# Attention and two gated layers on one core: folded weights of batches 4 to 7 made per head through DRAM, the attention pool split in two, Silu written with Tanh

## The chip, the cores and the metric

The kernel runs on 1 core of one Trainium2 chip. The metric is device time in microseconds (us), the median of several runs; the profile is one execution of the same program with its own time.

## The reference, cut to what matters

```
a    = softmax over the sequence of phi            # 8 batches, 8 heads, 576 positions, 32 memories
k_m, v_m = a^T k, a^T v                            # per head 32 x 64
attn = softmax(q k_m^T / 8) ; x = attn v_m         # per head 576 x 64
x = (silu(x @ w_gate) * (x @ w_val)) @ w_out       # 4608 x 512, 512 x 1536, 1536 x 512
h = x @ w_in ; g = where(h > 0, h, exp(min(h,0)) - 1)
out = g @ w_out2                                   # 512 x 2048, 2048 x 512
```

All is float32; weights arrive as float64.

## The kernel before, in words

**Precision.** Each matrix is split in a high and a low part (`fp32r`), and each product is three matmuls: high by high, high by low, low by high.

**Folding.** The kernel never forms x. For each batch and each pair of 128-column units p (0 to 5) of the first layer, `vw` (L112) multiplies the batch's `v_m` (block-diagonal, transposed: `vt`) by the gate and value columns `WG[p]`. That takes two groups g of six matmuls with 512 columns, one PSUM tile each, then a copy (L124) and a difference (L125) into `VW[b, p]`. `gate1` and `val1` (L148, L155) multiply `VW` by the attention matrix `at`, 288 positions at a time: six matmuls of 288 columns each.

**Loop 1** (L406) goes over the 8 batches with units u = 0 to 3 (p = 0, 1) and writes the partial result `p1` of the down product to DRAM. Between its matmuls `tick` gives out tasks of a list: the front of the attention of batch b+2 (k_m and v_m), the back of batch b+1 (scores, softmax, transposes), and `vw` of batch b+1. Everything of the attention lies in one pool, `at_p`, which is closed after iteration 6, when the pools `wb` and the PSUM of loop 2 are opened and the weights of p = 2 to 5 and of u = 4 to 11 are asked for (L440 to L457).

**Loop 2** (L512) goes over the 8 batches and two halves with units u = 4 to 11: `gate1`, `val1`, the down product of the unit two before (`down2`), and one piece of `vw` of the next batch from `vwq`. Each half ends with an addition to `p1` and a store to DRAM. Late in loop 2 the weights of the third part are asked for (L527, L534, L540 to L543).

**Part 3** (L594) is the last layer: 9 tiles of 512 tokens by 16 units, each 24 matmuls of 512 columns, with Exp and Tanh on ScalarE (L568, L569).

**A weight load** (`load_w`, L92) is a DMA of 512 KB and the splitting of float64 in two float32 parts (`split_w`, L71): two ScalarE copies (L77, L83), four VectorE operations (L78, L79, L81, L82) and two GpSimd operations (L84, L85). The raw tile `wr` and the value `v` have two buffers, the integer tile `c` has one:

```
v = wt_p.tile([128, 512], F32, tag="wv", name="wv", bufs=2)
c = wt_p.tile([128, 512], I32, tag="wc", name="wc")
```

**Order.** The order of the text is a priority: a scheduler with a timeline of its own places each instruction when its inputs and its buffer are there, so work can run ahead of its place in the text. All DMAs are issued from the one queue of SP, in order. A buffer in a pool is given out in turn, and the next tile in it waits for the readers of the last one.

Of the kernel before, what the change touches and what calls it, by code (L numbers as in the profile page):

```python
# [26 lines left out]
UA = 4  # L27
NCH = 5
NWA = 24
NWB = 32  # L30
NWC = 8
# [3 lines left out]
def attention_moe_moe(ctx: ExitStack, tc: tile.TileContext, qT, phiT, kv, w1g, w1o, w2, out):  # L35
# [10 lines left out]
    wt_p = ctx.enter_context(tc.tile_pool(name="wt", bufs=1))  # L46
# [14 lines left out]
    ps_at = st_ps.enter_context(tc.tile_pool(name="ps_at", bufs=2, space=PSUM))  # L61
    st_at = ExitStack()
    at_p = st_at.enter_context(tc.tile_pool(name="at", bufs=1))
# [3 lines left out]
    p1_d = [dram.tile([128, KD, S], F32, name=f"p1d{b}") for b in range(B)]  # L67
    x1_d = [dram.tile([128, KD, S], F32, name=f"x1d{b}") for b in range(B)]


    def split_w(raw, hi, lo):  # L71
        lo32, hi32 = raw[:, :, 0], raw[:, :, 1]
        v = wt_p.tile([128, 512], F32, tag="wv", name="wv", bufs=2)
# [74 lines left out]
    def gate1(b, u, at, s0):  # L148
        pg = ps_gv.tile([128, HS], F32, tag="g", name="pg")
        up1(pg, VW[b, u // 2], 256 * (u % 2), at, s0)  # L150
        s = t_p.tile([128, HS], F32, tag="s", name="s")
        act(out=s, in_=pg, func=AF.Silu)  # L152
        return s

    def val1(b, u, at, s0, s):  # L155
# [3 lines left out]
        tt(out=h, in0=s, in1=pv, op=ALU.mult)  # L159
# [3 lines left out]
    ident = at_p.tile([128, 128], F32, tag="ident", name="ident")  # L163
    make_identity(nc, ident)
    mask = at_p.tile([128, 4, 64], F32, tag="mask", name="mask")
# [14 lines left out]
    class Batch:  # L180
# [21 lines left out]
        def phi(self):  # L202
            ph = self.ph
            nmx = at_p.tile([128, 2], F32, tag="nmx", name="nmx")
            nc.vector.tensor_reduce(out=nmx, in_=ph, op=ALU.max, axis=AX.X, negate=True)
            sm = at_p.tile([128, 2], F32, tag="sm", name="sm")
# [3 lines left out]
            self.rs = at_p.tile([128, 2], F32, tag="rs", name="rs", bufs=2)  # L210
# [41 lines left out]
        def kv_out(self):  # L252
            self.kvm = at_p.tile([128, 2, 2, 256], F32, tag="kvm", name="kvm")
# [5 lines left out]
        def k_T(self):  # L259
# [4 lines left out]
            self.kT = at_p.tile([128, 2, 2, 128], F32R, tag="kT", name="kT")  # L264
# [26 lines left out]
        def score(self, c):  # L291
            n = chunk(c)
            if c == 0:
                self.sc = at_p.tile([128, NCH, 256], F32, tag="sc", name="sc")
# [6 lines left out]
            t = at_p.tile([128, 4, 64], F32, tag="sct", name="sct", bufs=2)  # L301
# [103 lines left out]
    wl = []  # L405
# [231 lines left out]
```

## Time and profile before

| | |
|---|---|
| time, median of 3 runs | 1793.68 us (1787.94 to 1795.11) |
| the profiled execution | 1791.92 us |
| its span, first to last instruction | 1790.1 us |
| TensorE matmul busy | 95% of the span |
| VectorE, ScalarE, GpSimd busy | 59%, 43%, 16% |
| mean granted clock of TensorE | 0.971 |

Busy time of TensorE is a sum over matmuls that overlap in the pipeline, so a matmul's own duration is longer than the time until the next one starts. Where an engine runs without a gap, the number of matmuls in a stretch says more than its busy share.

### The profile page before, as it was taken

To read this page: it belongs to the slowest core of one execution; us is meant where nothing else is said; L and a number is where in the kernel's file an instruction comes from. 1 tells how busy PE (TensorE), PEld (TensorE's weight loads), DVE (VectorE), ACT (ScalarE), POOL (GpSimd) and SP (SyncE) were. 2 spreads that over 40 slices of the span, in tenths; PEclk is the share of its full clock that TensorE was granted. 3 is DMA by queue.
4 is the path that set the end of the run, shared out by engine and by line. 5 is a ranking of instruction groups with operands and counts; after the bars stand their busy time and mean duration, and the time that the engine had idled before them with its cause. 6 is when DMAs were issued, how large, how long until landed. Compare 5 with 4: busy or idle time off the path is not lost.

```text
span 1790.1 us, 24102 instructions
## 1 busy us (share of the span) xinstructions
PE 1708.9 (95%) x9424; PEld 1496.5 (84%) x9424; DVE 1047.8 (59%) x1781; ACT 770.8 (43%) x1447; POOL 277.6 (16%) x197
## 2 busy tenths in 40 slices
PE   6689999999869999999999999999999999999998
PEld 4478998898759999999999878888888888888887
DVE  6887677657665333333368887455545555555554
ACT  5567666654433222322345444343434343434332
POOL 3552222114442000000034441000000000000000
PEclk8779999999969999999999999999999999999999
DMA  6555444234434121112225221010101010101000
GB/s 217 181 183 192 155 158 155 65 116 148 139 104 166 54 66 66 67 52 79 67 75 169 92 83 48 1 48 0 48 1 48 1 48 1 47 1 47 1 24 24
DMA packets 68209, 144.68 MB, mean 81 GB/s; under 512 B 7168, under 2 KB 38912, under 8 KB 66048
## 3 DMA queue, kind: packets, MB, share of 16 engines
q1 hardware_dynamic: 68096, 143.16, 24.1%
q8 instruction: 73, 1.20, 0.3%
q14 instruction: 40, 0.33, 0.1%
HBM read 101.19 MB, written 41.94 MB: 80 GB/s over the span
## 4 chain that ended last, share of the span: by engine, by line
PE 78%; DVE 9%; DMA 4%; ACT 3%; issue 2%; POOL 2%; SPq 0%; ACTq 0%; POOLq 0%; DVEq 0%
PE acc L581 7%; PE acc L582 7%; PE acc L583 7%; PE pu L557 7%; PE pu L555 6%; PE pu L556 6%; PE acc L139 3%; PE acc L138 3%; PE acc L137 3%; PE pg L132 2%; PE pv L132 2%; PE pg L133 2%; PE pg L134 2%; PE pv L134 2%; PE pv L133 2%
## 5 line engine op out<-in xcount | busy, mean ns | idle before, releaser
L581 PE MATMUL acc<-whi,hh 128*128 128x512 f32 x576 | 224.8, 390 | 3.3 <-ACT hh L143 3.3
L555 PE MATMUL pu<-x1s,whi 128*128 128x512 f32 x576 | 224.2, 389 | 1.6 <-DVE g L571 1.6
L582 PE MATMUL acc<-wlo,hh 128*128 128x512 f32 x576 | 224.2, 389 | 0.0
L557 PE MATMUL pu<-x1s,wlo 128*128 128x512 f32 x576 | 224.1, 389 | 0.0
L556 PE MATMUL pu<-x1s,whi 128*128 128x512 f32 x576 | 224.1, 389 | 0.0
L583 PE MATMUL acc<-whi,hl 128*128 128x512 f32 x576 | 223.0, 390 | 0.0
L570 DVE SCALAR_TENSOR_TENSOR g<-e,g 128x512 f32<-128x512 f32 x144 | 104.8, 727 | 157.1 <-ACT g L569 156.9
L84 POOL TENSOR_TENSOR wv<-wv,whi 128x512 f32<-128x512 f32 x68 | 102.1, 1501 | 587.3 <-ACT whi L83 469.6
L143 ACT ACTIVATE hh<-g 128x512 fp32r<-128x512 f32 x144 | 90.9, 632 | 217.0 <-DVE g L571 212.4
L159 DVE TENSOR_TENSOR h<-s,pv 128x288 f32<-128x288 f32 x192 | 86.5, 451 | 164.5 <-PE pv L134 135.3
L568 ACT ACTIVATE e<-g 128x512 f32<-128x512 f32 x144 | 90.8, 631 | 205.5 <-DVE g L567 205.2
L138 PE MATMUL acc<-hh,wlo 128*128 128x288 f32 x512 | 151.7, 298 | 2.7 <-POOL wlo L85 2.7
L145 DVE TENSOR_TENSOR hl<-g,hh 128x512 fp32r<-128x512 f32 x144 | 100.3, 697 | 87.0 <-ACT hh L143 87.0
L139 PE MATMUL acc<-hl,whi 128*128 128x288 f32 x512 | 149.7, 298 | 0.7 <-DVE hl L145 0.7
L137 PE MATMUL acc<-hh,whi 128*128 128x288 f32 x512 | 150.1, 296 | 0.3 <-ACT hh L143 0.3
L145 DVE TENSOR_TENSOR hl<-h,hh 128x288 fp32r<-128x288 f32 x192 | 108.4, 565 | 61.7 <-ACT hh L143 61.2
L143 ACT ACTIVATE hh<-h 128x288 fp32r<-128x288 f32 x192 | 85.0, 443 | 124.4 <-DVE h L159 123.9
L152 ACT ACTIVATE s<-pg 128x288 f32<-128x288 f32 x192 | 78.1, 408 | 123.6 <-PE pg L134 122.6
L581 PEld LDWEIGHTS acc<-whi,hh 128*128 128x128 f32 x576 | 108.1, 188 | 27.8 <-ACT hh L143 5.7
L567 DVE TENSOR_SCALAR g<-pu 128x512 f32<-128x512 f32 x144 | 99.3, 689 | 53.5 <-PE pu L557 53.3
L555 PEld LDWEIGHTS pu<-x1s,whi 128*128 128x128 f32 x576 | 108.1, 188 | 24.3 <-DVE g L571 2.0
L583 PEld LDWEIGHTS acc<-whi,hl 128*128 128x128 f32 x576 | 107.9, 187 | 24.5 <-DVE hl L145 2.2
(107 smaller groups left out, 4084.1 us busy)
## 6 DMA issues: line engine op xcount, KB each, us to landing
kvr<-kv SPq DMA_DIRECT2D x32, 512.0 KB, 3.9
wr<-w SPq DMA_DIRECT2D x32, 512.0 KB, 3.5
wr<-w1g SPq DMA_DIRECT2D x24, 512.0 KB, 3.6
atd<-at SPq DMA_DIRECT2D x8, 1152.0 KB, 4.9
p1d<-p SPq DMA_DIRECT2D x64, 144.0 KB, 2.0
p1l<-p1d SPq DMA_DIRECT2D x16, 576.0 KB, 4.1
at<-atd SPq DMA_DIRECT2D x8, 1152.0 KB, 5.2
x1d<-p1l SPq DMA_DIRECT2D x16, 576.0 KB, 3.3
```

Source lines behind the costliest of these rows:

```text
L137: mm(ps, lhsT=w[0][:, ms], rhs=hs[0], start=start, stop=False)
L138: mm(ps, lhsT=w[1][:, ms], rhs=hs[0], start=False, stop=False)
L139: mm(ps, lhsT=w[0][:, ms], rhs=hs[1], start=False, stop=stop)
L143: act(out=hh, in_=h, func=AF.Copy)
L145: tt(out=hl, in0=h, in1=hh.bitcast(F32), op=ALU.subtract)
L555: mm(ps, lhsT=wh[:, k, :], rhs=xh, start=k == 0, stop=False)
L556: mm(ps, lhsT=wh[:, k, :], rhs=xl, start=False, stop=False)
L557: mm(ps, lhsT=wl[:, k, :], rhs=xh, start=False, stop=k == KD - 1)
L570: stt(out=g, in0=e, scalar=1.0, in1=g, op0=ALU.add, op1=ALU.mult)
L581: mm(accs[c], lhsT=hs[0][:, cs], rhs=wh, start=u == 0, stop=False)
L582: mm(accs[c], lhsT=hs[0][:, cs], rhs=wl_, start=False, stop=False)
L583: mm(accs[c], lhsT=hs[1][:, cs], rhs=wh, start=False, stop=u == NU2 - 1)
```

## The change

Three things are done.

1. **Per-head folding for batches 4 to 7** (`NM` = 4). In loop 2 the folded weights of batches 0 to 3 are made as before. For batches 4 to 7, one matmul makes those of all four batches for one head (64 rows of the weights): the 128 columns of the stationary side are 4 batches by 32 memories, and the 128 rows are the head's 64 rows twice, once against the high and once against the low part of the weights. A second matmul adds the low part of `v_m` by the high part of the weights. `load_vq` gathers `v_m` from DRAM in 48 DMAs with runs of 128 bytes, `load_wf` builds the stacked weights with four DMAs from SBUF to SBUF, `fold` makes the two matmuls, a copy and a store to DRAM, and `load_vw` reads the folded weights back, one DMA for each batch and p, and splits them.
2. **Pools.** The attention pool becomes `fr_p` (front) and `bk_p` (back). The front is closed after iteration 5 of loop 1 instead of 6; the weights of loop 2 are given out as tasks inside iterations 6 and 7, with `spread` 24 instead of 12, and two `vw` of batch 0 as well. `wt_p` gets two buffers, so `c` too. The weights of part 3 are asked for in batches 1, 3 and 4 of loop 2 (17 loads), the other 15 at its end.
3. **Silu.** `gate1` computes (tanh(g/2) + 1) g with one more VectorE operation, and `val1` multiplies by one half.

```diff
-NWB = 32
-NWC = 8
+NWB = 22
+NWD = 4
+NWC = 18
+NM = 4
...
-    wt_p = ctx.enter_context(tc.tile_pool(name="wt", bufs=1))
+    wt_p = ctx.enter_context(tc.tile_pool(name="wt", bufs=2))
...
+    vw_d = {p: dram.tile([128, B - NM, 2, 512], F32, name=f"vwd{p}") for p in range(UA // 2, NU1 // 2)}
...
-        act(out=s, in_=pg, func=AF.Silu)
+        act(out=s, in_=pg, func=AF.Tanh, scale=0.5)
+        stt(out=s, in0=s, scalar=1.0, in1=pg, op0=ALU.add, op1=ALU.mult)
...
-        tt(out=h, in0=s, in1=pv, op=ALU.mult)
+        stt(out=h, in0=s, scalar=0.5, in1=pv, op0=ALU.mult, op1=ALU.mult)
...
+        if b == B - 2:
+            wb_p = ctx.enter_context(tc.tile_pool(name="wb", bufs=NWB))
+            ps_vw = ctx.enter_context(tc.tile_pool(name="ps_vw", bufs=1, space=PSUM))
+            fr += wg_tasks(2, wb_p)
+            fr += wg_tasks(3, wb_p)
+        if b == B - 1:
+            fr.append(lambda: load2(0))
+            fr += wg_tasks(4, wa_p)
+            fr += [lambda: load_wo(4, wb_p), lambda: vw2(0, 2)]
+            fr += wg_tasks(5, wa_p)
+            fr += [lambda: load_wo(5, wb_p), lambda: vw2(0, 3), lambda: load_wo(6, wb_p)]
...
+        spread = 12 if b < B - 2 else 24
...
-            upto = min(len(todo), -(-len(todo) * (done[0] + 3) // 12))
+            upto = min(len(todo), -(-len(todo) * (done[0] + 3) // spread))
...
-        if b == B - 2:
-            st_at.close()
+        if b == B - 3:
+            st_fr.close()
             st_ps.close()
-            wb_p = ctx.enter_context(tc.tile_pool(name="wb", bufs=NWB))
-            for p in range(2, 5):
-                for k in range(KD):
-                    load_wg(p, k, wb_p)
-                if p < 4:
-                    for u in (2 * p, 2 * p + 1):
-                        load_wo(u, wb_p)
...
+    load_wo(7, wa_p)
+    for u in (8, 9):
+        load_wo(u, wd_p)
+    for u in (10, 11):
+        load_wo(u, wa_p)
...
+    def load_vq():
+        for r in range(2):
+            o = slice(64 - 64 * r, 128 - 64 * r)
+            nc.gpsimd.memset(vq[o, 1, :, r].bitcast(F32), 0.0)
+        for b in range(NM, B):
+            for r in range(2):
+                rows = slice(64 * r, 64 * r + 64)
+                for c in range(2):
+                    col = 32 * (2 * c + r)
+                    src = vt_d[b][rows, :, c::2, col:col + 32].bitcast(F32)
+                    for half in range(2):
+                        nc.sync.dma_start(out=vq[64 * half:64 * half + 64, 0, c::2, r, b - NM, :].bitcast(F32),
+                                          in_=src[:, 0])
+                    nc.sync.dma_start(out=vq[rows, 1, c::2, r, b - NM, :].bitcast(F32), in_=src[:, 1])
+
+    def load_wf(p, k):
+        t = wf_p.tile([128, 2, 512], F32R, tag="wf", name="wf")
+        for r in range(2):
+            rows, other = slice(64 * r, 64 * r + 64), slice(64 - 64 * r, 128 - 64 * r)
+            nc.sync.dma_start(out=t[rows, r].bitcast(F32), in_=WG[p][k][0][rows].bitcast(F32))
+            nc.sync.dma_start(out=t[other, r].bitcast(F32), in_=WG[p][k][1][rows].bitcast(F32))
+        WF[p, k] = t
+
+    def fold(p, k, r):
+        w = WF[p, k][:, r]
+        ps = ps_vw.tile([128, 512], F32, tag="vw", name="pvq")
+        mm(ps, lhsT=vq[:, 0, k, r].rearrange("p b m -> p (b m)"), rhs=w, start=True, stop=False)
+        mm(ps, lhsT=vq[:, 1, k, r].rearrange("p b m -> p (b m)"), rhs=w, start=False, stop=True)
+        io = io_p.tile([128, 512], F32, tag="io", name="vwo")
+        act(out=io, in_=ps, func=AF.Copy)
+        r0 = 32 * (2 * (k % 2) + r)
+        nc.sync.dma_start(out=vw_d[p][r0:r0 + 32, :, k // 2, :].rearrange("m b f -> b m f"), in_=io)
+
+    def load_vw(b, p):
+        t = VW[b, p] = vx_p.tile([128, 2, 2, 512], F32R, tag="vx", name="vwl")
+        nc.sync.dma_start(out=t[:, 1].bitcast(F32), in_=vw_d[p][:, b - NM])
+        for g in range(2):
+            act(out=t[:, 0, g], in_=t[:, 1, g].bitcast(F32), func=AF.Copy)
+            tt(out=t[:, 1, g], in0=t[:, 1, g].bitcast(F32), in1=t[:, 0, g].bitcast(F32), op=ALU.subtract)
...
+    for p in (4, 5):
+        vw2(0, p)
+    load_vq()
+
+    when = {(1, 0): 2, (2, 0): 3, (3, 0): 4, (3, 1): 5}
+    heads = [(p, k, r) for p in range(UA // 2, NU1 // 2) for k in range(KD) for r in range(2)]
+    load_wf(*heads[0][:2])
+    w2q = [(1, wa_p)] + [(3, wb_p)] * 8 + [(4, wa_p)] * 8
...
+                if (b, hf) in when:
+                    p, k, r = heads.pop(0)
+                    if r == 0 and len(heads) > 1:
+                        load_wf(*heads[1][:2])
+                    fold(p, k, r)
...
-                    if b + 1 < B:
-                        vwq += [(b + 1, u // 2, 0), (b + 1, u // 2, 1)]
+                    if b + 1 < NM:
+                        vwq += [(b + 1, u // 2, (g,)) for g in range(2)]
+                    elif b + 1 < B:
+                        load_vw(b + 1, u // 2)
...
-                if b == 2 and hf == 0 and u % 2:
-                    more_w2(wa_p, 1)
+                if u % 2 == 0 and w2q and w2q[0][0] <= b:
+                    more_w2(w2q.pop(0)[1])
```

## Rows read from the trace of the kernel before

**Rows 1.** The page: busy time, share of the span and instructions.

```profile
PE 1708.9 (95%) x9424; PEld 1496.5 (84%) x9424; DVE 1047.8 (59%) x1781; ACT 770.8 (43%) x1447; POOL 277.6 (16%) x197
```

**Rows 2.** Stretches: length, busy (instructions) by engine, clock, DMA share, GB/s.

```profile
322.00:369.00 47.00, 46.05 (x319) 42.72 (x318) 28.63 (x59) 28.24 (x60) 10.80 (x8) 1.00 0.26 88
...
405.00:570.00 165.00, 138.08 (x848) 124.33 (x847) 106.62 (x193) 67.17 (x146) 72.02 (x52) 0.90 0.41 136
570.00:985.00 415.00, 415.00 (x2902) 401.90 (x2901) 183.09 (x370) 138.68 (x297) 37.62 (x26) 1.00 0.25 81
985.00:1095.00 110.00, 104.68 (x471) 83.93 (x470) 94.37 (x145) 54.00 (x91) 43.48 (x30) 1.00 0.23 75
1095.00:1784.00 689.00, 689.00 (x3041) 570.38 (x3039) 372.87 (x550) 262.29 (x422) 0.00 (x0) 1.00 0.07 23
```

**Rows 3.** Stretches of 15 us inside 405 to 570, the same columns.

```profile
480.00:495.00 15.00, 10.42 (x42) 8.53 (x43) 8.56 (x16) 4.89 (x10) 6.81 (x5) 0.67 0.31 101
...
510.00:525.00 15.00, 7.86 (x25) 5.87 (x25) 9.05 (x13) 4.67 (x9) 6.36 (x5) 0.61 0.31 104
```

**Rows 4.** Waits of PE, 405 to 570: us in total, times, longest.

```profile
PE pvw L123 <- POOL wlo L85: 7.1, 5, 1.9
PE pvw L121 <- ACT whi L83: 6.5, 4, 2.6
```

**Rows 5.** Waits of DVE, 405 to 570.

```profile
DVE wc L78 <- POOL wlo L85: 33.5, 20, 3.7
```

**Rows 6.** Timeline of POOL: start, us; the first and the 24th load.

```profile
393.72 1.29 POOL L84 TENSOR_TENSOR wv<-wv,whi 128x512 f32<-128x512 f32 x1 [27.11 <-DVE at L337]
...
530.20 1.29 POOL L84 TENSOR_TENSOR wv<-wv,whi 128x512 f32<-128x512 f32 x1 [3.54 <-ACT whi L83]
```

**Rows 7.** Groups on DVE, 405 to 480: count, busy us, mean ns, idle before.

```profile
L82 DVE SCALAR_TENSOR_TENSOR wc<-wr,wc 128x512 f32<-128x512 uint32 x13 | 11.1, 854 | 0.4
L79 DVE SCALAR_TENSOR_TENSOR wv<-wv,wc 128x512 int32<-128x512 int32 x12 | 8.3, 691 | 0.3
...
L81 DVE TENSOR_SCALAR wc<-wv 128x512 int32<-128x512 int32 x13 | 5.5, 422 | 0.1
L78 DVE TENSOR_SCALAR wc<-wv 128x512 int32<-128x512 int32 x12 | 5.1, 425 | 11.5 <-POOL wlo L85 11.4
```

**Rows 8.** Timeline of the DMA queue of SP.

```profile
356.63 0.32 SPq L280 DMA_DIRECT2D vtd<-vt  x1
...
463.97 2.94 SPq L403 DMA_DIRECT2D p1d<-p  x4
...
697.68 0.54 SPq L475 DMA_DIRECT2D p1l<-p1d  x1
...
759.78 0.54 SPq L475 DMA_DIRECT2D p1l<-p1d  x1
```

**Rows 9.** Groups on DVE, 590 to 900.

```profile
L145 DVE TENSOR_TENSOR hl<-h,hh 128x288 fp32r<-128x288 f32 x80 | 36.6, 457 | 33.2 <-ACT hh L143 33.2
L159 DVE TENSOR_TENSOR h<-s,pv 128x288 f32<-128x288 f32 x80 | 36.4, 455 | 113.2 <-PE pv L134 97.4 <-ACT vw L124 15.8
L125 DVE TENSOR_TENSOR vw<-pvw,vw 128x512 fp32r<-128x512 f32 x40 | 27.6, 690 | 50.9 <-ACT vw L124 50.9
L486 DVE TENSOR_TENSOR p1l<-acc,p1l 128x288 f32<-128x288 f32 x40 | 16.3, 449 | 0.0
```

**Rows 10.** Group on DVE, 910 to 985, while POOL splits weights.

```profile
L145 DVE TENSOR_TENSOR hl<-h,hh 128x288 fp32r<-128x288 f32 x19 | 16.6, 871 | 3.0 <-ACT hh L143 2.8
```

**Rows 11.** Groups on ACT: table loads of Silu, 150 to 395.

```profile
L152 ACT ACT_TABLE_LOAD x9 | 11.5, 1283 | 0.2
```

**Rows 12.** Groups of the whole span: the table load ahead of part 3.

```profile
L568 ACT ACT_TABLE_LOAD x1 | 1.3, 1283 | 0.0
```

**Rows 13.** Waits of PE, 140 to 405.

```profile
PE pv L132 <- ACT s L152: 3.6, 1, 3.6
```

**Rows 14.** Line L94, the raw weight DMAs of 512 KB.

```profile
DMA to landing us min/median/max: 3.0/3.6/7.2
```

More of the change, by code (lines that the diff above doesn't have):

```diff
@@ L60, in attention_moe_moe @@
     ps_fr = st_ps.enter_context(tc.tile_pool(name="ps_fr", bufs=1, space=PSUM))
-    ps_at = st_ps.enter_context(tc.tile_pool(name="ps_at", bufs=2, space=PSUM))
-    st_at = ExitStack()
-    at_p = st_at.enter_context(tc.tile_pool(name="at", bufs=1))
+    st_pa = ExitStack()
+    ps_at = st_pa.enter_context(tc.tile_pool(name="ps_at", bufs=2, space=PSUM, side="right"))
+    st_bk, st_fr = ExitStack(), ExitStack()
+    bk_p = st_bk.enter_context(tc.tile_pool(name="bk", bufs=1, side="right"))
+    fr_p = st_fr.enter_context(tc.tile_pool(name="fr", bufs=1))
     at_d = [dram.tile([128, 2, 2, S], F32R, name=f"atd{b}") for b in range(B)]
@@ L72, in split_w @@
         lo32, hi32 = raw[:, :, 0], raw[:, :, 1]
-        v = wt_p.tile([128, 512], F32, tag="wv", name="wv", bufs=2)
+        v = wt_p.tile([128, 512], F32, tag="wv", name="wv")
         c = wt_p.tile([128, 512], I32, tag="wc", name="wc")
@@ L403, in down1, with load2, vw2, wg_tasks @@
         nc.sync.dma_start(out=p1_d[b][:, m, HS * hf:HS * hf + HS], in_=io)
-    wl = []
+    at2, vt2 = {}, {}
+    def load2(b):
+        if b < NM:
+            vt2[b] = av_p.tile([128, 2, KD, 128], F32R, tag="vt", name="vt2")
+            nc.sync.dma_start(out=vt2[b].bitcast(F32), in_=vt_d[b].bitcast(F32))
+        at2[b] = av_p.tile([128, 2, 2, S], F32R, tag="at", name="at2")
+        nc.sync.dma_start(out=at2[b].bitcast(F32), in_=at_d[b].bitcast(F32))
+    def vw2(b, p, gs=(0, 1)):
+        vw(b, p, vt2[b], ps_vw, "vw", gs)
+    def wg_tasks(p, pool):
+        for k in range(KD):
+            yield lambda k=k: load_wg(p, k, pool)
     for b in range(B):
@@ L450, in attention_moe_moe @@
     st_p1 = ExitStack()
     p1_p = st_p1.enter_context(tc.tile_pool(name="p1", bufs=1, side="right"))
-    load_wo(8, wa_p)
-    load_wo(9, wa_p)
-    for k in range(KD):
-        load_wg(5, k, wa_p)
-    load_wo(10, wa_p)
-    load_wo(11, wa_p)
+    wd_p = st_p1.enter_context(tc.tile_pool(name="wd", bufs=NWD, side="right"))
+    vq_p = st_p1.enter_context(tc.tile_pool(name="vq", bufs=1, side="right"))
+    wf_p = st_p1.enter_context(tc.tile_pool(name="wf", bufs=2, side="right"))
+    load_wo(7, wa_p)
@@ L507, in attention_moe_moe @@
     pend = []
-    load2(0)
-    for p in range(UA // 2, NU1 // 2):
-        vw(0, p, vt2[0], ps_vw, "vw")
+    for p in (4, 5):
[5 more added lines that the diff above has]
+    w2q = [(1, wa_p)] + [(3, wb_p)] * 8 + [(4, wa_p)] * 8
     vwq = []
@@ L539, in attention_moe_moe @@
     st_r.close()
-    more_w2(wb_p, 4)
-    more_w2(wa_p, 4)
-    wc_p = ctx.enter_context(tc.tile_pool(name="wc", bufs=NWC))
-    more_w2(wc_p, 4)
+    more_w2(wb_p, 3)
+    more_w2(wa_p, 3)
+    wc_p = ctx.enter_context(tc.tile_pool(name="wc", bufs=NWC, side="right"))
+    more_w2(wc_p, len(todo2))
     h3_p = ctx.enter_context(tc.tile_pool(name="h3", bufs=4, side="right"))
```

58 lines of the change are left out of this document (26 added, 32 removed).

## The prediction, made before the changed kernel was run

> **What bounds the kernel now.** I read the page first, then the stretches, then the waits of the stretches that lose time. The page says that TensorE is busy for 95% of the span and no other engine over 59% [rows 1]. That share is a sum over stages, so the stretches come next. From 570 to 985 (loop 2) and from 1095 to the end (part 3) TensorE is busy for the whole of it [rows 2]: nothing but fewer matmuls makes these shorter. In loop 1 the stretch from 322 to 369 is 46.05 of 47. The loss lies in 405 to 570, where 848 matmuls ran. At the rate of the next stretch, 2902 in 415 us or 6.99 a microsecond, they take 121.3 us, so 43.7 us are lost, and the worst of it is 480 to 525, with 25 to 42 matmuls in 15 us and the granted clock at 0.61 to 0.67, near the lower of the two levels [rows 3]. TensorE there waits for parts of weights, from ScalarE and from GpSimd [rows 4]. Why the weights are late is seen on the other side: VectorE waited 33.5 us, 20 times, to write the one tile `c` because GpSimd still read it [rows 5], and 24 loads came at one in (530.20 - 393.72) / 23 = 5.93 us [rows 6]. The first could not start before the attention pool closed (the row of 393.72 waits for L337, the last step of the attention).
>
> **Price of a matmul.** With 512 columns 689 / 3041 = 0.2266 us [rows 2]. A batch of loop 2 takes 759.78 - 697.68 = 62.10 us [rows 8]; 48 of its matmuls have 512 columns, 10.9 us, and the other 384, with 288 columns, share 51.2 us: 0.1334 each.
>
> **The folding.** For batches 4 to 7 it takes out 4 batches by 4 p by 12 = 192 matmuls, 43.5 us, and adds 32 heads by 2 = 64, 14.5 us. Net -29.0 us, all of it in loop 2, where no gap hides it. Its copies (32 on ScalarE, one DMA trip through DRAM) run on engines that are under half busy: ScalarE 138.68 of 415, DMA 0.25 [rows 2]. What TensorE can wait for is the stacked weights: asked for two units ahead, 2 by 24 by 0.1334 = 6.4 us. No row shows a copy from SBUF to SBUF; the nearest is the raw weight DMA, landing in 3.0 to 7.2 us [rows 14], with issues of 0.32 to 0.54 [rows 8]. Four issues and a landing are 4.9 us at the middle, 9.4 at worst: no wait, or 3.0 us for each of 16 pairs, 48 in all. I take +2 us, since the middle is well under 6.4. The read back of `VW` has six units (19 us) before its use, and I price it at nothing; without that cover it would cost the same landing, 16 times.
>
> **The weights of loop 2.** They may start when batch 7's front is done, at about 357 (its last store, [rows 8]) where they started at 394. The second buffer of `c` takes away the 33.5 us wait, some 1.4 us a load. What then sets the pace? A load takes VectorE 0.425 + 0.691 + 0.422 + 0.854 = 2.39 us [rows 7] and GpSimd two operations like the 1.29 us of [rows 6]. Two raw buffers give 3.3 us at best (3.6 landing, 0.67 for the first copy taken like L79, 2.39, over two). A unit of loop 1 keeps VectorE for 0.455 + 0.457 [rows 9] and one new operation like L159, 0.455, so 1.37 of its 3.2 us. The rest, 57%, gives 2.39 / 0.57 = 4.2 us a load. I take 4.7, with the folding's VectorE work, between 3.3 and today's 5.93. Eight loads fit before 400. The ninth writes into the buffers of p = 0, which are read until `vw` of batch 7, and `spread` 24 puts that near the end of iteration 6. Loop 1 now ends at about 464 [rows 8], a few microseconds of waits among it; so say 460, and an iteration is 192 by 0.1334 + 24 by 0.2266 = 31 us, so `vw` of batch 7 is at about 425. Sixteen loads from there end at 425 + 75 = 500. The last is wanted after ten units and two foldings, 460 + 32 + 5 = 497. I leave 6 of the 43.7 us: -37.7. Bounds: nothing left if the scheduler runs that `vw` earlier (-43.7), 23 left if the pace stays at 5.93 (-20.7).
>
> **The queue of SP.** 48 small DMAs and 64 for the stacks, 16 to 36 us of issue at 0.32, are spread over loop 1's end and loop 2. Behind a waiting raw load stand stores of `p1` and loads that are wanted tens of microseconds later. Covered, so 0; uncovered it is the last rival.
>
> **Silu.** 192 more VectorE operations, nearest row L159 with one input in PSUM, 0.455: 87 us if nothing hid them. In loop 1 VectorE goes from 28.63 to 32.3 of 47 us, in loop 2 it has 183 of 415: hidden. In return ScalarE loses its table loads (nine of 1.283 us for Silu alone between 150 and 395, [rows 11]; Exp and Tanh together need one in the whole of part 3, [rows 12]). TensorE waited only 3.6 us behind them [rows 13]. I take -1, bounds -3.6 and +2.
>
> **Weights of part 3.** Moving 16 loads into batches 3 and 4 is where VectorE gets tight. A batch of loop 2 costs it 16 (0.455 + 0.457) + 8 by 0.690 + 8 by 0.449 = 23.7 us [rows 9], and now 7.3 more and 8 by 2.39 = 19.1: 50.1, against 51.2 of TensorE in batch 4 and 58.5 in batch 3 (32 fold matmuls). And while GpSimd splits, `hl` took 0.871 instead of 0.457 [rows 9, 10], 6.6 us a batch: 56.7 against 51.2. I take +5, bounds 0 and +11. At the start of part 3, 471 matmuls in 110 us where the full rate needs 106.7: 3.3 lost, and more loads come ahead of time, so -2 (+3 to -3.3).
>
> The Trainium skill, "GPSIMD Engine Reference", section "8. Key points", says that GpSimd shares its SBUF interfaces with VectorE and contends with VectorE instructions that have two SBUF inputs. The trace agrees for `hl`, which has two: 0.871 against 0.457. By that rule, GpSimd working more densely slows the very operations that feed it, and the pace would stay near 5.93: that is the first rival below, 1744 instead of 1727.
>
> **Before loop 1** the 12 first loads have the same wait: 12 by 1.4 = 17 us if all lay on the path, but attention work fills VectorE there. I take -2, bounds -8 (half, the attention taking the rest) and +2 (four new operations of 0.455).
>
> **Sum.** -29.0 + 2 - 37.7 - 1 + 5 - 2 - 2 = -64.7 us. The profiled execution took 1791.9 (span 1790.1 and 1.8 around it), 1.8 under the median shown: 1727 us.
>
> **The rivals.**
> - *The loads stay at 5.93 us*, VectorE being held by GpSimd. For: `hl` above. Against: the 33.5 us wait is plainly the one buffer. 17 us more: 1744. Chance 0.20.
> - *The scheduler runs ahead*: `vw` of batch 7 early, all weights in time, the start gains its 8. For: it did so before (weights were split as soon as the pool closed). Sum of the good ends about -80: 1712. Chance 0.17.
> - *VectorE becomes the bound in batches 1 to 4*: +11 for the loads and 15 more for the stacks arriving late, instead of 7 in all: 1746 to 1755, say 1750. For: 56.7 against 51.2. Against: today's 16 loads in batches 6 and 7 cost nothing to see. Chance 0.13.
> - *Nothing to show*: the fold saving is eaten by these waits and the gap stays, because the late `vw` of batch 7 holds the weights. About 1788. It needs both; chance 0.02.
> - *Slower*: SP's queue, in order, holds each stack of weights behind a store or a raw load that waits, and TensorE, also in order, stands before each pair of folds. From 64.7 / 16 = 4.0 us a pair beyond my 2 us in all it ends slower than before; at 6 us, 1727 + 94 = 1821. For: four DMAs a stack in one queue, raw loads in batch 3. Against: the worst landing gives 3.0 us a pair. Chance 0.04.
>
> The forecast itself has 0.44. Its own range is 1715 to 1740. The range that leaves out no more than 2 in 10 reaches from the second rival to the third, with the unknown ends: 1706 to 1762. Half a per cent, 9 us, is about what this measurement can tell from no change: faster 0.44 + 0.20 + 0.17 + 0.13 = 0.94, same 0.02, slower 0.04.
>
> **What would show it.** Batches 4 to 7 of loop 2 at 51 us each where 62 stood, and 64 matmuls of the new kind. First weight of loop 2 split near 360, loads at 4 to 5 us, no wait of L78 on L85. The clock at 1.00 through the change of loops, matmuls near 105 in each 15 us there. No table load after the first. VectorE over 90% in batches 3 and 4, with some waits of TensorE for `hh`. It is wrong if TensorE waits for the stacks at folds, if the weights start no earlier than now, or if the start of loop 1 moves by more than 10 us.

## The result, and the profile after

The changed kernel takes 1808.86 us (median of 5, 1802.36 to 1811.5), the kernel before 1788.7 us (median of 5, 1786.54 to 1795.11): 1.0101 times as long [1.0082, 1.0119]. The forecast was 1727 us, faster. The profiled execution took 1805.48 us, with a span of 1803.7.

The page's line of busy times, as in [rows 1]:

```profile
PE 1684.5 (93%) x9296; PEld 1475.7 (82%) x9296; DVE 1155.3 (64%) x1973; ACT 750.8 (42%) x1455; POOL 284.5 (16%) x199
```

128 matmuls fewer (9424 to 9296), so the folding is there, and TensorE is busy for 24.4 us less. The span is 13.6 us longer all the same: TensorE stands still more.

The stretches, with the columns of [rows 2]:

```profile
405.00:570.00 165.00, 149.92 (x983) 139.47 (x982) 118.11 (x207) 67.43 (x147) 47.50 (x34) 0.98 0.45 138
...
355.00:405.00 50.00, 42.98 (x264) 38.03 (x264) 48.22 (x87) 24.05 (x56) 25.12 (x19) 0.93 0.39 132
675.00:825.00 150.00, 117.76 (x724) 108.61 (x723) 92.67 (x172) 52.03 (x112) 35.39 (x26) 0.90 0.55 167
```

and in the kernel before:

```profile
355.00:405.00 50.00, 50.00 (x347) 47.12 (x347) 29.90 (x64) 27.98 (x65) 8.77 (x7) 1.00 0.32 118
```

The gap of 405 to 570 did get smaller (983 matmuls where 848 stood). But there are two new ones: 355 to 405, where VectorE is busy for 48.22 of 50 us (29.90 before), and 675 to 825, where TensorE is busy for 117.76 of 150 us. No other engine is full over the whole of that second gap, but VectorE is in a part of it: 28.57 of 30 us in 690 to 720, and 12.31 in 720 to 750.

Where the time went is read best from the stores of `x1`, one at the end of each half of a batch of loop 2. The second, tenth and sixteenth on SP's queue, before:

```profile
569.88 0.56 SPq L487 DMA_DIRECT2D x1d<-p1l  x1
...
818.52 0.54 SPq L487 DMA_DIRECT2D x1d<-p1l  x1
...
1000.86 0.55 SPq L487 DMA_DIRECT2D x1d<-p1l  x1
```

and after:

```profile
555.85 0.55 SPq L558 DMA_DIRECT2D x1d<-p1l  x1
...
849.71 0.54 SPq L558 DMA_DIRECT2D x1d<-p1l  x1
...
1012.90 0.54 SPq L558 DMA_DIRECT2D x1d<-p1l  x1
```

They cut the span into four parts: to the end of batch 0 of loop 2, batches 1 to 4 (all the folds), batches 5 to 7, and part 3 (below, each row is rounded so that it adds up). The forecast by these parts is worked out from its own terms: batches 1 to 4 lose the 96 matmuls of `vw` for batches 4 and 5 and gain 64, 32 by 0.2266 = -7.3, and have its +2 and +5; batches 5 to 7 lose the other 96, -21.8; the start has -37.7, -1 and -2; part 3 has -2.

| us | to batch 0 | batches 1 to 4 | batches 5 to 7 | rest | span |
|---|---|---|---|---|---|
| before | 569.9 | 248.6 | 182.4 | 789.2 | 1790.1 |
| forecast | 529.2 | 248.3 | 160.6 | 787.2 | 1725.4 |
| after | 555.9 | 293.8 | 163.2 | 790.8 | 1803.7 |
| after less forecast | +26.7 | +45.5 | +2.6 | +3.6 | +78.3 |

So two parts failed: the start gave 14 us instead of 41, and batches 1 to 4 cost 45 instead of nothing. In the third part the saving of the folding arrived whole: the stores of batches 4, 5 and 6 lie at 849.71, 900.40 and 951.28, 50.8 us a batch as forecast.

The operations of a weight load on VectorE, 353 to 490, as in [rows 7]:

```profile
L87 DVE SCALAR_TENSOR_TENSOR wc<-wr,wc 128x512 f32<-128x512 uint32 x19 | 19.4, 1023 | 0.2
L84 DVE SCALAR_TENSOR_TENSOR wv<-wv,wc 128x512 int32<-128x512 int32 x19 | 15.7, 827 | 0.1
L83 DVE TENSOR_SCALAR wc<-wv 128x512 int32<-128x512 int32 x19 | 14.3, 755 | 8.3 <-ACT wv L82 8.2
L86 DVE TENSOR_SCALAR wc<-wv 128x512 int32<-128x512 int32 x19 | 11.1, 582 | 0.1
```

The 33.5 us wait of [rows 5] is gone, as meant. But one load now keeps VectorE for 1.023 + 0.827 + 0.755 + 0.582 = 3.19 us, where the same four took 2.39. The work is the same; its operations have become longer.

In 675 to 825, the largest waits of PE, and two of ACT (us in total, times, longest):

```profile
PE pg L137 <- ACT vwl L535: 10.3, 1, 10.3
PE pvq L524 <- ACT vwo L527: 9.1, 2, 4.9
PE pv L137 <- DVE s L159: 7.8, 8, 3.1
...
ACT whi L88 <- DMA wf<-whi: 26.7, 6, 6.6
ACT vwl L535 <- DMA vwl<-vwd: 14.2, 3, 12.8
```

and the timelines of ACT and then of PE:

```profile
740.04 0.63 ACT L88 ACTIVATE whi<-wv 128x512 fp32r<-128x512 f32 x1 [6.56 <-DMA wf<-whi]
...
763.63 0.63 ACT L88 ACTIVATE whi<-wv 128x512 fp32r<-128x512 f32 x1 [5.39 <-DMA wf<-whi]
764.17 0.58 ACT L527 ACTIVATE vwo<-pvq 128x512 f32<-128x512 f32 x1
...
764.80 0.80 PE L524 MATMUL pvq<-wf,vq 128*128 128x512 f32 x1 [4.16 <-ACT vwo L527]
```

ScalarE stands for 6.56 and 5.39 us at `whi`, the copy that splits a weight of part 3. The buffer that it is to write still holds a weight of loop 2 that the transfer of a stack (`wf`) is reading. Behind it on ScalarE stand `hh`, the gate and `vwo`, the copy that empties the fold's PSUM tile: TensorE's next fold waits 4.16 us for that copy. A load for part 3, which begins some 270 us later, holds up work that is wanted now.

### The profile page after: what moved, and what is told of

The parts are those of the page before. It is cut to its first block, busy times and chain, and to the rows that moved or that the text cites. A ratio compares the mean times of both kernels' runs of the same rounds, so it can differ in the third digit from the quotient of the medians.

```text
span 1803.7 us, 24336 instructions
## 1 busy us (share of the span) xinstructions
PE 1684.5 (93%) x9296; PEld 1475.7 (82%) x9296; DVE 1155.3 (64%) x1973; ACT 750.8 (42%) x1455; POOL 284.5 (16%) x199
## 4 chain that ended last, share of the span: by engine, by line
PE 63%; DVE 16%; issue 12%; DMA 6%; ACT 2%; SPq 1%; POOL 1%; DVEq 0%; POOLq 0%; ACTq 0%
PE acc L663 7%; PE acc L662 7%; PE acc L661 7%; PE pu L637 7%; PE pu L636 7%; PE pu L635 7%; DVE wc L87 2%; DVE wv L84 2%; DVE wc L83 2%; DVE hl L150 2%; PE acc L142 2%; PE acc L143 2%; PE acc L144 2%; PE pg L137 1%; PE pv L137 1%
## 5 line engine op out<-in xcount | busy, mean ns | idle before, releaser
L650 DVE SCALAR_TENSOR_TENSOR g<-e,g 128x512 f32<-128x512 f32 x144 | 100.6, 699 | 160.2 <-ACT g L649 160.2
L648 ACT ACTIVATE e<-g 128x512 f32<-128x512 f32 x144 | 90.8, 631 | 221.8 <-DVE g L647 221.8
L144 PE MATMUL acc<-hl,whi 128*128 128x288 f32 x512 | 144.3, 299 | 5.0 <-DVE hl L150 4.9
L159 DVE SCALAR_TENSOR_TENSOR s<-s,pg 128x288 f32<-128x288 f32 x192 | 85.8, 448 | 90.6 <-ACT s L158 90.2
L647 DVE TENSOR_SCALAR g<-pu 128x512 f32<-128x512 f32 x144 | 99.3, 689 | 56.7 <-PE pu L637 56.6
L662 PEld LDWEIGHTS acc<-wlo,hh 128*128 128x128 f32 x576 | 108.4, 188 | 22.7
```

The source lines that it names most:

```text
L144: mm(ps, lhsT=w[0][:, ms], rhs=hs[1], start=False, stop=stop)
L662: mm(accs[c], lhsT=hs[0][:, cs], rhs=wl_, start=False, stop=False)
```

## The experiments

Four parts of each profiled span, as in the table above, and the ratio of its times to those of the kernel before. The theories 1 to 3 are those of the expectations.

| kernel | to batch 0 | 1 to 4 | 5 to 7 | rest | median us | ratio |
|---|---|---|---|---|---|---|
| after | 555.9 | 293.8 | 163.2 | 790.8 | 1808.9 | 1.0101 [1.0082, 1.0119] |
| a1_w2_late | 556.0 | 298.1 | 163.3 | 790.7 | 1806.4 | 1.0099 [1.0078, 1.0120] |
| a2_c_one_buffer | 540.0 | 283.7 | 160.2 | 782.6 | 1768.0 | 0.9889 [0.9855, 0.9923] |
| a3_silu_back | 559.5 | 292.9 | 160.1 | 792.5 | 1807.1 | 1.0095 [1.0071, 1.0120] |
| a4_no_heads | 554.4 | 248.0 | 204.5 | 789.4 | 1800.8 | 1.0066 [1.0043, 1.0089] |
| b1_c_two_buffers | 570.3 | 248.3 | 203.9 | 789.0 | 1814.1 | 1.0142 [1.0120, 1.0165] |
| a5_w2_held | 552.2 | 275.0 | 164.4 | 794.6 | 1787.0 | 0.9991 [0.9978, 1.0004] |
| a6_w2_held_c_one | 540.2 | 274.0 | 156.1 | 788.8 | 1762.9 | 0.9856 [0.9831, 0.9881] |
| a7_no_heads_c_one | 539.2 | 247.0 | 189.3 | 798.6 | 1773.3 | 0.9915 [0.9891, 0.9939] |
| a8_folds_early | 541.8 | 267.7 | 156.6 | 788.8 | 1754.7 | 0.9811 [0.9792, 0.9831] |
| a9_folds_early_w2_free | 541.0 | 289.8 | 160.2 | 782.8 | 1775.4 | 0.9926 [0.9903, 0.9949] |
| a10_three_stacks | 544.6 | 261.8 | 156.4 | 789.0 | 1749.9 | 0.9787 [0.9766, 0.9809] |
| a11_v_one_buffer | 542.2 | 275.4 | 155.7 | 787.7 | 1765.3 | 0.9872 [0.9850, 0.9894] |

**The weights of part 3 asked for later** (batches 5 and 6).

```diff
-    w2q = [(1, wa_p)] + [(3, wb_p)] * 8 + [(4, wa_p)] * 8
+    w2q = [(1, wa_p)] + [(5, wb_p)] * 8 + [(6, wa_p)] * 8
```

> The changed kernel with the 16 weight loads of part 3 asked for in batches 5 and 6 instead of 3 and 4. Theory 1: the changed kernel loses its time in batches 3 and 4 because ScalarE, which is in order, stands at the copies of these loads until the DMAs for the stacked weights have read the buffers that the copies write (ScalarE waited 26.7 us there). Then most of the 45 us lost in batches 2 to 4 comes back: 1765 to 1780. Theory 2: the hand-over of the folds itself (four DMAs, a store and a read for each p) is what is late. Then batches 3 and 4 stay as long and the time stays at 1800 to 1810. Theory 3, VectorE full: the loss moves with the loads to batches 5 and 6, and no more than 10 us come back.

Nothing moved, and for a plain reason: these 16 loads are issued at 671 to 795 us, in the changed kernel at 672 to 789. The scheduler starts a load when its buffers come free, though the text here asks for it two batches later. The run tells the theories apart by nothing; a5 below does what it was meant to do.

**One buffer for c.**

```diff
-        c = wt_p.tile([128, 512], I32, tag="wc", name="wc")
+        c = wt_p.tile([128, 512], I32, tag="wc", name="wc", bufs=1)
```

> The changed kernel with one buffer for the integer tile c, as before. If the second buffer is what gave the 14 us by which loop 2 now starts earlier, the weights of loop 2 come at 5.9 us again and the time rises by 10 to 20 us. If VectorE is held by GpSimd when loads follow each other closely (a load cost it 3.19 us instead of 2.39 between 353 and 490), then it is the same or faster, by up to 10 us.

40 us back, four times what the second theory allowed, and the kernel is faster than the one before: the second buffer, which the prediction counted as the gain, was the largest loss. It costs 16 us in the start, 10 in batches 1 to 4, 3 in 5 to 7 and 8 in the rest. The operations of a load on VectorE in this run, 353 to 490:

```profile
L87 DVE SCALAR_TENSOR_TENSOR wc<-wr,wc 128x512 f32<-128x512 uint32 x16 | 12.2, 766 | 0.2
L84 DVE SCALAR_TENSOR_TENSOR wv<-wv,wc 128x512 int32<-128x512 int32 x16 | 11.0, 685 | 0.1
L83 DVE TENSOR_SCALAR wc<-wv 128x512 int32<-128x512 int32 x17 | 7.9, 463 | 13.3 <-ACT wv L82 8.2 <-POOL wlo L90 5.1
L86 DVE TENSOR_SCALAR wc<-wv 128x512 int32<-128x512 int32 x16 | 6.8, 422 | 0.2
```

Together 2.34 us instead of 3.19. For 19 loads that is 16 us of VectorE, the size of the gain in the start. The weights themselves come no earlier for it: GpSimd begins the 24th load of loop 2 at 511.7 us here and at 507.05 in the changed kernel. What is won back is the work of loop 1 beside them.

**Silu as before.**

```diff
-        act(out=s, in_=pg, func=AF.Tanh, scale=0.5)
-        stt(out=s, in0=s, scalar=1.0, in1=pg, op0=ALU.add, op1=ALU.mult)
+        act(out=s, in_=pg, func=AF.Silu)
...
-        stt(out=h, in0=s, scalar=0.5, in1=pv, op0=ALU.mult, op1=ALU.mult)
+        tt(out=h, in0=s, in1=pv, op=ALU.mult)
```

> The changed kernel with Silu again. If the additional VectorE operation, standing behind the operations of weight loads, is what makes TensorE wait for the value half (19.3 us in 16 waits), the time falls by 10 to 25 us in loop 1's last iterations and in batches 3 and 4. If the table loads of Silu cost as much as they save VectorE, it stays within 5 us; slower by up to 10 if ScalarE is what is late in batches 3 and 4.

In all, no difference that can be measured. But the two kernels run differently in loop 1: the table loads return (47 in this run, 1 in the changed kernel), by 320 us 1550 matmuls have run instead of 1621, and the first weight of loop 2 is split at 380.6 us instead of 351.87. The end of batch 0 comes only 3.6 us later all the same, and the later parts make up for that. So the run does not settle theory 3, since 192 operations leave VectorE while table loads come to ScalarE, and no run shows what Tanh is worth with one buffer for `c`.

**No heads** (all eight batches folded as before, the loads of part 3 asked for as before; two buffers for c stay).

```diff
-NM = 4
+NM = 8
...
-    when = {(1, 0): 2, (2, 0): 3, (3, 0): 4, (3, 1): 5}
+    when = {}
...
-    w2q = [(1, wa_p)] + [(3, wb_p)] * 8 + [(4, wa_p)] * 8
+    w2q = [(1, wa_p)]
```

> The changed kernel with the folding of all batches as before, no stacks, no trip through DRAM, and the weights of part 3 asked for in batch 6 as before; pools, two buffers and Tanh stay. If the per-head folding with its buffers is the whole of the loss in loop 2, loop 2 takes its 431 us again instead of 457 and the 14 us at its start stay: 1770 to 1782. If the other two parts lose as well, it is at 1790 or above.

Batches 1 to 4 are whole again (248.0), but the loads of part 3 now stand in batches 6 and 7, which go from 182.4 to 204.5: with two buffers for c, weights cost time wherever they are split. The second theory of the expectation holds: the other two parts lose as well. Folding by heads is 8 us worse than not folding, in this surrounding.

**The second buffer of c alone, in the kernel before.**

```diff
-        c = wt_p.tile([128, 512], I32, tag="wc", name="wc")
+        c = wt_p.tile([128, 512], I32, tag="wc", name="wc", bufs=2)
```

> The kernel before with a second buffer for the tile c, and nothing else of the change. The prediction's own step says that this is worth some 1.4 us a load: 24 loads by 1.4 us is up to 34 us of the 43.7 us lost between 405 and 570, so about 1755 to 1765 us. Theory H (VectorE is held while GpSimd works, and the second buffer makes the two work at the same time): the loads take no less time in all and other VectorE work is held as well, so the time is 1785 to 1830 us, with the operations of a load in 405 to 570 above the 2.39 us that they take now. Theory O (the second buffer lets the order on VectorE pack load operations ahead of the gates; the length of an operation does not matter): 1785 to 1830 us too, but with the operations of a load still at 2.4 us.

25 us slower, nothing else being changed. The loads do come faster: 28 of them between 410.57 and 542.59 us, one in 4.89, against the 5.93 of [rows 6], close to the 4.7 that the prediction took. Yet the end of batch 0 stays where it was: by 320 us 1550 matmuls have run where 1595 had, with 45 table loads in the span instead of 25, all the additional ones before 407 us, so in the start a changed order of the work may have a part in it. Batches 6 and 7, where both kernels split weights and load no table but the one for part 3, lose 21 us by themselves. There, before:

```profile
910.00:1000.00 90.00, 89.57 (x618) 86.03 (x617) 71.19 (x128) 43.87 (x91) 43.15 (x30) 1.00 0.42 135
```

and with two buffers:

```profile
910.00:1000.00 90.00, 79.07 (x511) 73.42 (x510) 84.81 (x122) 40.26 (x86) 50.46 (x35) 0.96 0.42 137
```

VectorE is busy for 84.81 of 90 us instead of 71.19, with fewer operations. Its groups with two buffers, 405 to 570:

```profile
L79 DVE SCALAR_TENSOR_TENSOR wv<-wv,wc 128x512 int32<-128x512 int32 x28 | 33.6, 1200 | 0.6
L78 DVE TENSOR_SCALAR wc<-wv 128x512 int32<-128x512 int32 x28 | 26.9, 961 | 5.9 <-ACT wv L77 5.6
L82 DVE SCALAR_TENSOR_TENSOR wc<-wr,wc 128x512 f32<-128x512 uint32 x28 | 24.0, 858 | 0.6
L81 DVE TENSOR_SCALAR wc<-wv 128x512 int32<-128x512 int32 x28 | 12.4, 445 | 0.3
```

L78 went from 0.425 to 0.961 and L79 from 0.691 to 1.200: a load costs VectorE 3.46 us. Theory H says why, and the timelines show it. VectorE:

```profile
449.21 1.78 DVE L79 SCALAR_TENSOR_TENSOR wv<-wv,wc 128x512 int32<-128x512 int32 x1
450.92 0.44 DVE L159 TENSOR_TENSOR h<-s,pv 128x288 f32<-128x288 f32 x1
451.28 1.14 DVE L81 TENSOR_SCALAR wc<-wv 128x512 int32<-128x512 int32 x1
...
456.23 0.69 DVE L79 SCALAR_TENSOR_TENSOR wv<-wv,wc 128x512 int32<-128x512 int32 x1
456.84 0.45 DVE L145 TENSOR_TENSOR hl<-h,hh 128x288 fp32r<-128x288 f32 x1
457.20 0.42 DVE L81 TENSOR_SCALAR wc<-wv 128x512 int32<-128x512 int32 x1
```

and POOL:

```profile
448.83 1.61 POOL L84 TENSOR_TENSOR wv<-wv,whi 128x512 f32<-128x512 f32 x1 [3.03 <-ACT whi L83]
450.52 1.61 POOL L85 TENSOR_TENSOR wlo<-wv,wc 128x512 fp32r<-128x512 f32 x1
```

While GpSimd works (448.83 to 452.13), L79 takes 1.78 and L81 1.14; with GpSimd idle, 456.23 to 457.6, the same two take 0.69 and 0.42. L159, which reads PSUM, takes 0.44 in the middle of GpSimd's work. Sorted over 405 to 570 by whether more than half of an operation lay inside one of GpSimd's: L78 1.142 us (21 of them) against 0.419 (7), L79 1.638 (15) against 0.693 (13), `hl` 1.353 (11) against 0.450 (23), `h` 0.443 (12) against 0.446 (21). In the kernel before all 26 of L78 and all 26 of L79 lie outside. There the one buffer made VectorE wait for GpSimd's last operation before it began the next load, and kept the two engines apart for these steps: the 33.5 us of waiting in [rows 5] bought undisturbed operations. It did not do so for all: 14 of 27 L82 and 11 of 31 `hl` lay inside GpSimd's in the kernel before too, at 1.07 and 1.02 us.

**The loads of part 3 held back** to batches 4 to 7, each bound behind a copy of `hh`.

```diff
-    w2q = [(1, wa_p)] + [(3, wb_p)] * 8 + [(4, wa_p)] * 8
+    w2q = [(1, wa_p)] + [(4, wb_p)] * 8 + [(6, wa_p)] * 8
...
-                if u % 2 == 0 and w2q and w2q[0][0] <= b:
-                    more_w2(w2q.pop(0)[1])
+                if u % (2 if b < 4 else 4) == 0 and w2q and w2q[0][0] <= b:
+                    with tc.issue_after(HH[0].ins):
+                        more_w2(w2q.pop(0)[1])
```

> The changed kernel with the 16 moved loads of part 3 held back: the first 8 in batches 4 and 5, the other 8 in batches 6 and 7, one in four units, each bound to its place behind a copy of hh on ScalarE, so that they cannot move ahead to where the folds are. Theory 1 (the folds' stacks come late because the weights of part 3 are split beside them: ScalarE and SP stand at copies into buffers that are not yet free): batches 2 and 3 fall from 76 and 92 us to 65 or less, the later batches keep 51 to 53 us each, and the time is 1765 to 1780 us. Theory 2 (the hand-over of a stack to a fold is late by itself): batches 2 and 3 stay above 74 and 85, 1795 to 1815 us. Theory 3 (VectorE is full wherever a weight is split): the loss moves with the loads to batches 4 to 7, 1795 to 1815 us, with batches 5 to 7 at 55 us or more.

1787.0 us, above theory 1's range and below that of the others: it is right in kind, and half in size. Batches 2 and 3 come to 69.0 and 76.4 us, not to 65. Batches 1 to 4 fall by 18.8 us and batches 5 and 6 stay at about 52 us each, so the loads beside the folds cost that much; the rest of the span takes 3.8 us more. The run takes ScalarE's waits at `whi` and VectorE's work on these loads out of the same batches, so it does not tell the two apart. 33.7 us above the full rate (241.3, as worked out above without the +7) are left.

**The same with one buffer for c.** (Both edits above.)

> The same, and c with one buffer. If the two causes add up (40 us measured for the second buffer, of which 11 were in batch 3, and 30 to 40 us for the loads beside the folds), the time is 1735 to 1755 us, below the kernel before by 2 to 3%. If they are one cause, seen twice, it is that of one buffer alone, about 1768 us.

1762.9 us, outside the range of adding up and 5 below a2: in batches 1 to 4 the two causes are largely the same one seen twice (holding the loads is worth 18.8 us with two buffers, 9.7 with one). The largest wait of PE that is left there, 600 to 800:

```profile
PE pg L138 <- ACT vwl L536: 10.9, 1, 10.9
```

**No heads, one buffer for c** (a4 and a2 together).

> The changed kernel with all eight batches folded as before (no heads, no trip through DRAM), the weights of part 3 asked for as before, and c with one buffer: what is left of the change is the attention pool in two parts with the earlier weights, and Silu from Tanh. If the earlier weights are worth what the gap between 405 and 570 held, some 20 us of gain or more is left: 1755 to 1770 us. If the earlier weights only move the gap into loop 1, 1780 to 1795 us. The difference to the run with one buffer and heads (1768 us) is what the heads are worth, -29 us of matmuls and what they wait for.

1773.3 us, between the two ranges: the attention pool in two parts, the earlier weights and Tanh together are worth 0.85%, the start 30.7 us less than before. No run separates Tanh from the other two here. The heads, -29 us of matmuls, are worth 5 us in a2, 10 with a6's order, and 23 with a10's below.

**The folds brought forward**, to give the read back of batch 4 more time.

```diff
-    when = {(1, 0): 2, (2, 0): 3, (3, 0): 4, (3, 1): 5}
+    when = {(1, 0): 2, (1, 1): 3, (2, 0): 4, (2, 1): 5}
```

> The run with one buffer for c and the loads of part 3 held, and in it the folding of p = 3, 4 and 5 brought forward, to batch 1 second half, batch 2 first half and batch 2 second half (it was batch 2, 3 first half and 3 second half). Theory R (what was left between 690 and 780 us, some 20 us of TensorE standing, is the read back through DRAM of batch 4, asked for while the last folds still write): the waits of pg for vwl, 10.9 us once, are gone, batches 3 and 4 come to 60 and 52 us, and the time is 1740 to 1750 us. Theory 2 (a fold's hand-over costs by itself): the loss moves into batches 1 and 2 with the folds, 1758 to 1768 us.

1754.7 us, 8 below a6 and between the two ranges. The wait of `pg` for `vwl` is gone and batch 4 comes to 51.6 us, as theory R has it. But batch 3 takes 71.4, not 60, batch 2 goes from 69.1 to 85.2, where the folds moved into it are 3.6 us of matmuls, and only 6.3 us come off batches 1 to 4: part of the loss moved with the folds, as theory 2 has it.

**The same with the loads of part 3 free again.** (The hold is left out.)

> The same, but with the loads of part 3 as in the changed kernel, free to move ahead beside the folds. If the loads beside the folds cost by VectorE and ScalarE being shared (18 us were measured with the folds late and two buffers, 5 with one buffer), the time is 5 to 18 us above the run with the loads held. If they only hurt because they met the read back of batch 4, within 3 us of it.

20.7 us more than a8, over the upper range (22.1 in batches 1 to 4, with 6.0 given back in the rest): beside the folds these loads cost that much even with one buffer for c and with the read back out of the way. Stretches of this run:

```profile
690.00:720.00 30.00, 19.46 (x101) 17.75 (x102) 13.30 (x26) 9.44 (x19) 8.22 (x6) 0.77 0.39 116
...
750.00:780.00 30.00, 26.21 (x186) 24.71 (x186) 29.23 (x52) 15.05 (x33) 12.25 (x8) 1.00 0.59 201
```

and the same two of a8:

```profile
690.00:720.00 30.00, 27.27 (x167) 24.08 (x166) 10.91 (x24) 9.03 (x19) 0.00 (x0) 1.00 0.32 98
...
750.00:780.00 30.00, 30.00 (x229) 30.00 (x228) 22.18 (x46) 12.00 (x27) 5.18 (x4) 1.00 0.35 124
```

In the four stretches of 30 us from 660 to 780 this run falls 18, 66, 66 and 43 matmuls behind a8. In the first two VectorE is busy for 13.7 and 13.3 of 30 us and ScalarE for less, so neither is full there; in the last VectorE is, with 29.23. ScalarE and then TensorE in the second:

```profile
693.98 0.66 ACT L82 ACTIVATE wv<-wr 128x512 f32<-128x512 f32 x1 [8.28 <-DMA wr<-w]
694.55 0.58 ACT L129 ACTIVATE vw<-pvw 128x512 fp32r<-128x512 f32 x1
...
695.18 0.61 PE L137 MATMUL pg<-at,vw 128*128 128x288 f32 x1 [7.59 <-ACT vw L129]
```

ScalarE stands 8.28 us at the first copy of a load, `wv` from `wr`, waiting for a raw weight that comes late beside the stacks; the copy of `vw` stands behind it, and TensorE waits 7.59 us for that. From 660 to 790 it stands so nine times, 30.4 us: the queue on ScalarE again, with another transfer in front. So theory 1 holds in a wider form, in which ScalarE, in order, stands at a step of a load that waits for a transfer, and theory 3 can account for a smaller part, where VectorE is full.

**Three buffers for the stacks**, each asked for one pair earlier (on top of a8).

```diff
-name="wf", bufs=2, side="right"))
+name="wf", bufs=3, side="right"))
...
     load_wf(*heads[0][:2])
+    load_wf(*heads[2][:2])
...
-                    if r == 0 and len(heads) > 1:
-                        load_wf(*heads[1][:2])
+                    if r == 0 and len(heads) > 3:
+                        load_wf(*heads[3][:2])
```

> The run with folds brought forward and loads held, and with three buffers for the stacked weights, each asked for one pair earlier. If TensorE or the queue of SP still stands for a stack, 3 us or more are gained; if stacks are in time with two buffers, as the prediction took it at +2 us, no difference within 3 us.

1749.9 us, the best here: 0.9787 [0.9766, 0.9809] of the kernel before. The medians of a8 and this run differ by 4.7 us, and their ranges overlap by one. In a8 PE has a wait that is not there any more in this run:

```profile
PE pvq L525 <- DMA wf<-wlo: 6.5, 2, 3.8
```

So the stacks were late by about 6 us. What TensorE still waits for in batches 1 to 4, 540 to 810, and a wait of ScalarE there:

```profile
PE pg L138 <- ACT vw L130: 4.8, 7, 0.7
PE pvw L127 <- ACT vwo L528: 3.8, 7, 1.8
PE pvq L525 <- ACT vwo L528: 1.5, 2, 1.2
PE pvw L127 <- DVE vw L131: 1.0, 1, 1.0
...
ACT vwo L528 <- DMA vwd<-vwo: 16.6, 6, 4.6
```

`pvw` and `pvq` share the one buffer of `ps_vw`, so a fold beside a `vw` waits until ScalarE has copied the other out. The last row shows that ScalarE in turn stands at `vwo`, until the store of an earlier fold has read the buffer that the copy is to write. Neither a second buffer of `ps_vw` nor more buffers for `vwo` was tried, so both are argued from the rows and not shown. TensorE's 11 us are half of the 20.5 that are left over the full rate; the other half stays open.

**One buffer for v in place of one for c** (the changed kernel, c with two).

```diff
-        v = wt_p.tile([128, 512], F32, tag="wv", name="wv")
+        v = wt_p.tile([128, 512], F32, tag="wv", name="wv", bufs=1)
```

> The changed kernel with two buffers for c as it has them, and one buffer for v in place of two. GpSimd's last operation of a load reads v, so ScalarE may not write the next v, and VectorE not begin the next load, until GpSimd is done: the overlap of the two engines on weights is taken away by another tile than c. Theory H (overlap with GpSimd is what costs): VectorE's operations of a load fall from 3.19 us to under 2.7 in 353 to 490 us, and the time comes near the run with one c, 1765 to 1785 us. Theory O (it is the place of c in memory or the order that it gives, not the overlap): the time stays at 1800 us or rises.

1765.3 us. With c as in the changed kernel, and the overlap taken away by another tile, all of a2's gain is there. VectorE's operations of a load, 353 to 490, come to 0.949 + 0.688 + 0.470 + 0.441 = 2.55 us:

```profile
L87 DVE SCALAR_TENSOR_TENSOR wc<-wr,wc 128x512 f32<-128x512 uint32 x17 | 16.1, 949 | 0.3
L84 DVE SCALAR_TENSOR_TENSOR wv<-wv,wc 128x512 int32<-128x512 int32 x16 | 11.0, 688 | 1.0
L86 DVE TENSOR_SCALAR wc<-wv 128x512 int32<-128x512 int32 x16 | 7.5, 470 | 0.2
L83 DVE TENSOR_SCALAR wc<-wv 128x512 int32<-128x512 int32 x16 | 7.1, 441 | 5.1 <-ACT wv L82 5.0
```

That is theory H; theory O, that it was the place of c or the order that it gives, falls. How much of the 40 us is the longer operations themselves, and how much is load operations that stand ahead of the gates on VectorE, no run separates: a2 and a11 take away both.

## Why the prediction was wrong

*Weights of loop 2 (-37.7).* The dates were right: the first load at 351.87 (forecast 357), the ninth at 424.71 after GpSimd stood 25.9 us for `vw` of batch 7 (forecast 425), the 24th at 507.05 (forecast 500). The first of them was luck, since two effects that the prediction does not have cancelled: the second buffer alone puts the front's last store at 380.1 us instead of 356.6 (b1), and Tanh takes 29 of that back (351.4, against 380.8 with Silu in a3). The pace was not right: 6.0 us a load for the first eight and 5.5 for the other sixteen, not 4.7. The step that failed is "The second buffer of `c` takes away the 33.5 us wait, some 1.4 us a load", with VectorE at 2.39 us a load. It counted the wait as lost time and the four operations as fixed. They became 3.19 us, and every one lies in the queue of the engine that also makes the gates of loop 1, whose last stores of `p1` came at 484 to 488 us instead of 464 to 467. With one buffer (a2) the start gains 30 us over the kernel before, with loads at 6 to 7 us each: the pace did not need to rise.

*The first rival* had the mechanism, VectorE held by GpSimd, the right evidence (`hl` in [rows 9, 10]) and nearly the pace. The Trainium skill, "GPSIMD Engine Reference", section "8. Key points", puts it more widely than the prediction quoted: contention with VectorE instructions that have two SBUF inputs or run in a two-port mode. The runs agree for L79 and `hl`, with two inputs (1.64 against 0.69, 1.35 against 0.45); L78, with one, was held as well (1.14 against 0.42), which fits the second kind, though no row here names the mode. The price was too small: 17 us for slower loads, and nothing for the gates behind them. It measured 40 us by a2, and 25 in the kernel before, which puts the time above the old one and not at 1744.

*Weights of part 3 beside the folds (+5), and stacks (+2).* 45 us were missed here. The step priced VectorE's share, 56.7 against 51.2 us a batch; by the stretches of a9 that can be the smaller part of it. It failed to ask, for each copy of a new load on ScalarE, which transfer has to land or to read its buffer first, and what stands behind it on ScalarE. From the runs, one change on top of the other in batches 1 to 4: 18.8 us for the loads beside the folds (a5), 1.0 for `c` (a6), 6.3 for the read back of batch 4 that was priced at nothing (a8), 5.9 for stacks that come late (a10). That is 32.0 of the 45.5. In another order the shares differ: `c` is worth 10 when it goes first (a2), the loads 22 when they go last (a9 against a8). The step "six units before its use" was wrong for the first batch alone: the last folds write until just before it is read.

*Slower through SP's queue* was near in kind, in-order queues and late stacks. TensorE did stand before its folds, 9.1 us in 675 to 825, but for ScalarE's `vwo` and not for the stacks; ScalarE stood for the transfers that read the weights into them. The price of an issue was too low: the 112 transfers of the stacks and of `vq` took 0.6 us each at the median, 82 us of SP's queue in all, where the prediction had 16 to 36.

*The folding (-29.0)* was right, 0.2266 us a matmul and 50.8 us a batch where its surroundings are quiet. *Silu (-1)* was right in the sum, no table load after the start and no difference in a3, but not in its working: Tanh moves the start of the loads by 29 us. *Before loop 1 (-2)* had the right sign by luck: by 320 us 1621 matmuls had run instead of 1595, some 4 us, but the second buffer, to which the step put the gain, takes 45 matmuls away there (1550 in b1), with one buffer it is 1622 (a2), and Tanh brings the gain (1550 with Silu in a3). The first gate of loop 1 moved from 73.3 to 90.8 us (72.9 in a2), more than the 10 us that the prediction named as a sign of being wrong. *The start of part 3 (-2)* gave nothing, +1.6.

Half of the miss (40.9 of 81.9 us) thus goes with the tile `c` when it is taken away first, and 24.1 when the loads are held first (a5 to a6). a10, the change without its second buffer and with loads, folds and stacks in their places, is 38 us under the kernel before, its span still 26 over the forecast's: 15 in the start, 13 or 14 in batches 1 to 4, 2 in part 3, and 4 better in batches 5 to 7. The 15 in the start are about what its 24th load comes later than forecast (515.1 against 500 us), as the first rival had it; no run tests that, and the cause of the 13 or 14 stays open.

## What to carry to other kernels

A wait for a buffer can be what keeps two engines apart that slow each other down: before it is removed, look at how long the waiting engine's operations take when they fall inside the other engine's and outside, and price the whole queue behind them at the longer time. For a transfer or load that is moved, list for each of its steps the last reader of the buffer that it writes, and what is queued behind it on that engine; an engine that is far from full can still hold the others up so. Work that a scheduler may start early is not moved by asking for it later: here it had to be bound to something.

## What the runs showed of the hardware

In the kernel before with two buffers for `c` (b1, 405 to 570), VectorE's operations on SBUF operands took, with GpSimd at work, 1.14 instead of 0.42 us (one input, L78) and 1.64 instead of 0.69 (two inputs, L79), while one with a PSUM input (L159) took the same 0.44. GpSimd was slowed as well: L84 took up to 1.84 us there, and 1.27 with VectorE idle (kernel before).
